# Two 32-byte fillings, a table product moved from GpSimd to VectorE, and three moved steps in a routed attention-and-experts kernel

## Chip, cores and metric

The kernel runs on one core of one Trainium2 chip. The metric is the time of one execution in device microseconds (us), the median of three runs. The profile is of one further execution.

## What is computed

Attention without a softmax (a sigmoid of scaled scores), a layer of eight experts in which every token goes to one expert, and a gated feed-forward layer that all tokens pass. Cut to what matters:

```python
scores = scale * np.matmul(q, k.transpose(0, 1, 3, 2)) - np.log(S)    # 4 x 12 heads, 448 x 448, head 64
attn = 1.0 / (1.0 + np.exp(-scores))
x = np.matmul(attn, v)                       # as x: 1792 tokens x 768
logits = normalized(x) @ normalized(expert_emb).T / tau
expert_idx = np.argmax(logits, axis=1)       # one of 8; gate_w is its softmax weight
for e in range(E):
    out[mask] = gate_w[mask, None] * (np.maximum(x[mask] @ w1[e], 0.0) @ w2[e])   # 768 -> 1024 -> 768
gate = 1.0 / (1.0 + np.exp(-(out @ w_gate)))                                     # 768 -> 1536
y = gate * (out @ w_val) @ w_out                                                 # 1536 -> 768
```

## The kernel before

**Stages.** Attention runs first (to about 157 us of the span), then the experts (to about 463 us), then the feed-forward layer. Each matrix product of the last two stages is made of three products of a number split in two parts, `hi` (rounded to the fast fp32 form, by ScalarE at L215) and `lo` (the rest, by VectorE at L216): hi·hi, lo·hi, hi·lo. Weights arrive by SyncE's DMA in `rawb`, and `split_next` splits one piece of 128x1536 into a ring of four `hi` and four `lo` buffers, one piece per step of TensorE's work. So each engine works through its instructions in the order in which the program writes them, and that order is laid out by hand.

**Which operands TensorE reads at once.** While one product streams its moving operand, the weights of the next are loaded. In `h` (L1022) the moving operand is the ring and the loaded one the tokens `xh`, `xl`. In `y` (L1006 to L1008) it is the ring and `hh`, `hl`. In `gv` (L1240 to L1242) it is `yT`, and the loaded one is the ring. In `o` (L1006 to L1008 again) it is the ring and `gh`, `gl`.

**Where tiles lie.** Pools stand one behind the other in a partition: `const`, `rawb`, the ring, `yT`, the small `ytp` (two buffers tagged "y") and the feed-forward's own from the left, and from the right end inward `xp` (`xg`, `xh`, `xl`), `rt` (the routing tables), `moe` (`hr`, `hh`, `hl`, `yo`) and `small` (`xTq`, `hTq`). A tile's row takes its bytes rounded up to 32. By their sizes, `rawb` begins at byte 21440, the ring at 70592, `yT` at 119744 and `gh` at 150464, all multiples of 64. `xh` begins at 220128, `hh` at 181344 and `xTq` at 170592, all 32 past a multiple of 64.

**Around the first tokens (175 to 260 us).** `place_c` makes the table `am` on VectorE and from it, by `spread` (L604) on GpSimd, the table `spi` of token numbers. `ids_all` sums it on TensorE (`psid`, L611) in the midst of the product `y` of tile 0, and VectorE copies the sums to `idx`, with which GpSimd fetches the tokens of tiles 2 and 3 (`gather`, L859, an indirect DMA into one of two `xg` buffers). In the loop over `y` of tile 1, at its second step, `front(2)` turns tile 2's tokens, `gate_d` sums the gates, and `own_rows` makes a small product `repid` (L742, two instructions), a VectorE copy (L750) and two GpSimd steps, `own_row` (L751) and `moves` (L752). After that loop comes `gather(4)`. At the end of the tile loop's first pass (p = 2) `table_rows` on VectorE makes the tables of the rows to be written, `y_out(0)` and `y_out(1)` scatter the first outputs, and all engines pass a branch round the code of seldom-used tiles (L1165). In the next pass (p = 3) `small_ids` and `gather_small` fetch the tokens of five small tiles, `xq` and `xz`, into the two `xg` buffers, `front_small` (L1099) turns them, and `gather(5)` stands between.

Of the kernel before, what the change touches and what calls it, by code (L numbers as in the profile page):

```python
# [10 lines left out]
F32 = mybir.dt.float32  # L11
# [6 lines left out]
ALU = mybir.AluOpType  # L18
# [4 lines left out]
D = H * HD  # L23
# [3 lines left out]
P = 128  # L27
# [12 lines left out]
NSTAT = 14  # L40
# [67 lines left out]
def routed_kernel(ctx: ExitStack, tc: tile.TileContext, kqP, vP, emb, tau, w1P, w2P, wffP, cst, out):  # L108
    nc = tc.nc
    V, A, G, T, SP = nc.vector, nc.scalar, nc.gpsimd, nc.tensor, nc.sync  # L110

    cpool = ctx.enter_context(tc.tile_pool(name="const", bufs=1))
# [106 lines left out]
    def split_next(ahead=None, hi_eng=None):  # L219
        i = done_split[0]  # L220
        if i >= len(order):
            return
        done_split[0] += 1
        parts[i] = split(raws[raw_of[i]], ring, i, hi_eng=hi_eng)
        j = next((j for j in range(i + 1, len(order)) if order[j][:2] == ("gv", 0) and order[j][2] in direct), None)
        if j == i + 1:
            f = order[j][2]
            for step in range(3):
                decode(f, step)
            if f + 2 in direct:  # L230
                decode_load(f + 2, stage64[f % 2], raws[raw_of[j + 2]])
        it = order[i]
        if i not in nxt:
            return
        free = [i]
        if it[0] in ("w1", "w2") and PA <= it[1] < PA + NA:

            free = [i - 1, i] if it[2] % 2 else []
            for z in free:
                (h_small if it[0] == "w1" else y_small)(it[1] - PA, order[z][2], raws[raw_of[z]])  # L240
        for z in free:
            if ahead is None:
                load(nxt[z])
            else:
                ahead.append(nxt[z])
# [8 lines left out]

    cs = cpool.tile([P, NCONST], F32, name="cs")

    def C(name, rows=P):
        a, b = _COLS[name]
        return cs[:rows, a:b]

    me = ExitStack()
    xp = me.enter_context(tc.tile_pool(name="xp", bufs=2, side="right"))
# [5 lines left out]
    def R(name, shape, dt=F32):  # L268
        return rp.tile(shape, dt, name=name)
# [25 lines left out]
    ids_h = cpool.tile([CP, NT], F16, name="ids_h")  # L295
# [179 lines left out]
    bc3 = lambda a, n: a.unsqueeze(2).to_broadcast([a.shape[0], a.shape[1], n])  # L475
    bct = lambda a, n: a.unsqueeze(1).to_broadcast([a.shape[0], n, a.shape[1]])
    TT, TS, RED = V.tensor_tensor, V.tensor_scalar, V.tensor_reduce

    mx = R("mx", [CP, NT])
    m2 = R("m2", [CP, NT])  # L480
    eq = R("eq", [CP, NT, E])
    oh = R("oh", [CP, NT, E], F16)
# [114 lines left out]
            T.matmul(ps[:, 0, 0:1], bm[:, t, :], am1[:, k, t : t + 1], start=(t == 0), stop=(t == nt - 1))  # L597
        V.tensor_copy(idx01[:, k : k + 1], ps[:, 0, 0:1])

    def spread(am, vals, name):  # L600
        ncol, n = am.shape[2], len(vals)
        r = R(f"sp{name}", [CP, NT, n, ncol], F16)
        for q, v in enumerate(vals):
            G.tensor_tensor(out=r[:, :, q, :], in0=am, in1=bc3(v, ncol), op=ALU.mult)  # L604
        return r.rearrange("p t a b -> p t (a b)")

    def gathered(b, r, name):
# [14 lines left out]
    am = R("am", [CP, NT, NCOL], F16)  # L622
# [44 lines left out]
    gp = {"f": R("gf", [P, NCOL])}  # L667
# [55 lines left out]
    def place_c():  # L723
        ky = R("ky", [P, NCOL], F16)
        V.tensor_copy(ky, tn)
        TT(out=s3, in0=oh, in1=bct(C("e16", CP), NT), op=ALU.mult)
        po = R("po", [CP, NT])
        RED(out=po, in_=s3, axis=AX.X, op=ALU.add)
        ab = R("ab", [CP, NT], F16)
        TT(out=ab, in0=ai, in1=po, op=ALU.add)  # L730
        TT(out=am, in0=bct(ky[:CP], NT), in1=bc3(ab, NCOL), op=ALU.is_equal)
        gp["i"] = spread(am, [ids_h], "i")

    def ids_all():
        ps = gathered(bm, gp["i"], "id")
# [12 lines left out]
    def own_rows():  # L748

        V.tensor_copy(own_row[:, NPAIR:], repeated(idf, "id"))  # L750
        G.tensor_copy(own_row[:, :NPAIR], idx[:, :NPAIR])  # L751
        G.tensor_scalar(out=moves, in0=own_row, scalar1=float(NK), scalar2=None, op0=ALU.is_lt)  # L752
# [103 lines left out]
    def gather(p):  # L856
        xg = xp.tile([P, D], F32, tag="xg", name=f"xg{p}")
        ids = idx01[:, p : p + 1] if p < 2 else idx[:, p : p + 1]
        G.indirect_dma_start(out=xg, out_offset=None, in_=xd if p else xd[: TE * CP],  # L859
                             in_offset=bass.IndirectOffsetOnAxis(ap=ids, axis=0))  # L860
        xg_t[p] = xg

    def front(p, later=None):
        xg = xg_t.pop(p)
        ps = slot(f"xTp{p}")
        psf = ps.rearrange("p a b -> p (a b)")
        for k in range(KD):
            T.transpose(psf[:, k * P : (k + 1) * P], xg[:, k * P : (k + 1) * P], ident)
        if 0 <= p - 1 - PA < NA or p == PZ + 3:
            turn_small(min(p - 1 - PA, NA), psf[:, D : D + 256])  # L870
        hi = xp.tile([P, D], F32R, tag="xh", name=f"xh{p}")
        lo = xp.tile([P, D], F32R, tag="xl", name=f"xl{p}", bufs=1)
        A.copy(hi, psf[:, :D])
        xg_t["T", p] = (hi, lo)
        rest = lambda: V.tensor_sub(lo, psf[:, :D], hi)
        if later is None:
            rest()
        else:
            later.append(rest)
# [186 lines left out]
    def y_scale(p):  # L1066
        yo_t[p] = mp.tile([P, 2, 384], F32, tag="yo", name=f"yo{p}")
        A.activation(yo_t[p], yp_t.pop(p)[:, :, :384], AF.Copy, scale=gate_s[:, p : p + 1])
# [16 lines left out]

    def gather_small():
        for name, n, ids in (("xq", P, idq), ("xz", RQ, idx[:RQ, NCOL - 1 : NCOL])):
            x = xp.tile([P, D], F32, tag="xg", name=name)[:n]
            G.indirect_dma_start(out=x, out_offset=None, in_=xd,
                                 in_offset=bass.IndirectOffsetOnAxis(ap=ids, axis=0))  # L1090
            xg_t[name] = x
# [177 lines left out]
    ytp = ctx.enter_context(tc.tile_pool(name="yt", bufs=2, reuse_waits="tile"))  # L1269
# [36 lines left out]
    for c in range(NW2):  # L1306
        y_chunk(1, c, part[c])
        if c == 1:
            front(2)
            gate_d()  # L1310
            own_rows()
            y_scale(0)
        split_next()
    y_scale(1)

    gather(4)
    YT0, DEC_GAP = 9, 2
    for p in range(2, NSTAT):
        k, r = divmod(p - 4, DEC_GAP)
        dec = r == 1 and 0 <= k < DEC_MOE  # L1320
        if r == 0 and k < DEC_MOE:
            decode_load(DEC_ORDER[DEC_ATT + k], dp.tile([P, 2 * CH], F32, tag="w64", name=f"w64_{k}"),
                        dp.tile([P, CH], F32, tag="w32", name=f"w32_{k}"))
        for c in range(NW1):
            h_chunk(p, c)
            if p == 2 and c == NW1 - 2:
                front(3)
            elif p == 3 and c == 0:
                turn(2)
                small_ids()  # L1330
                gather_small()
            split_next()
            if c == 1 and p - PZ in (0, 1, 3):
                small_step((0, 2, 0, 6)[p - PZ])
            if dec and c % 2 == 0:
                decode(DEC_ORDER[DEC_ATT + k], c // 2)
        if 2 < p < NSTAT - 2:
            gather(p + 2)
        if 3 < p + 1 < NSTAT:
            front(p + 1)  # L1340
        if p > 2:
            for c in range(NW2):
                y_chunk(p - 1, c)
                if c == 2 and YT0 < p <= YT0 + 4:
                    yT_unit(0, p - YT0 - 1)
                split_next()
                if c == 1 and PZ <= p < PZ + 4:
                    small_step((1, 3, 4, 7)[p - PZ])
                if c == 3 and p == PZ + 2:
                    small_step(5)  # L1350
                if dec and c == 1:
                    decode(DEC_ORDER[DEC_ATT + k], 2)
            y_out(p - 1)
        else:
            table_rows()
            y_out(0)
            y_out(1)
            tail = [yTp.tile([P, KD, 512], F32R, tag=f"yT{k}", name=f"tail{k}") for k in range(2)]
            tail += [dp.tile([P, 6, 512], F32, tag="w64", name="tail_w"),
                     dp.tile([P, CH], F32, tag="w32", name="tail_x"), slot("tail")]  # L1360
            tc.mark_branch_hint_location("beyond", hint='LikelyTaken', engines=[mybir.EngineType.PE])
            n_tiles = nc.values_load(tabs["n"], min_val=0, max_val=NPAIR)
            tail_tiles(NSTAT)
        if p > 2:
            turn(p)
        if p == 3:
            front_small()
            gate_e()
        if p in (4, 5, 6):
            (packed_a, packed_b, packed_c)[p - 4]()  # L1370
        if YT0 <= p < YT0 + 4:
            y_load(G, 0, p - YT0)
        if p == PZ - 2:
            decp.close()
            dp = decp.enter_context(tc.tile_pool(name="zw", bufs=1, side="right", reuse_waits="tile"))
            for k in range(3):
                load_small(k)
# [118 lines left out]
```

## Time and profile before

| | us |
|---|---|
| median of three runs (1007.59 to 1008.35) | 1008.24 |
| the profiled execution | 1004.97 |
| its span, first to last instruction | 1003.2 |
| TensorE busy with products | 986.2 (98%) |
| VectorE busy | 584.2 (58%) |
| ScalarE busy | 484.5 (48%) |
| GpSimd busy | 108.8 (11%) |

The profiled execution lies 3.3 us below the median. A busy TensorE is one with a product under way: how close together products start is seen only in the order of time. PE is TensorE, PEld its weight loads, DVE VectorE, ACT ScalarE, POOL GpSimd, SP SyncE; a q behind a name is the engine's sequencer.

### The profile page before, as it was taken

How to read it: one execution, taken by the hardware profiler on the slowest of the kernel's cores; microseconds unless marked ns; L12 is line 12 of the kernel's file. 1: busy time of each engine (PE TensorE's matmuls, PEld its weight loads, DVE VectorE, ACT ScalarE, POOL GpSimd, SP SyncE). 2: the span in 40 equal slices, each digit the busy share in tenths (PEclk: the TensorE clock that was granted, in tenths of full speed). 3: DMA queues.
4: the chain of work that ended last, by engine and by line, in shares of the span. 5: the costliest groups of instructions: out<-in, count | busy, mean ns of one | idle time of the engine just before them, and what ended most of it. 6: DMA issues, size and time to landing. Idle time of an engine off the chain costs nothing.

```text
span 1003.2 us, 15168 instructions
## 1 busy us (share of the span) xinstructions
PE 986.2 (98%) x6099; PEld 815.4 (81%) x6099; DVE 584.2 (58%) x660; ACT 484.5 (48%) x527; POOL 108.8 (11%) x102
## 2 busy tenths in 40 slices
PE   9999999898999999999999999999999999999998
PEld 4455556777877788889888899888899888899998
DVE  6877768778887777876588633333333333322652
ACT  6676776485666677775322422333322333322441
POOL 0011013403331121201000000000000000001000
PEclk9999999998999999999999999999999999999999
DMA  8999875556699974692668633333333323323640
GB/s 304 319 360 333 294 247 173 186 195 240 231 382 319 317 287 156 214 326 78 231 211 295 215 109 114 130 100 105 135 106 117 130 100 106 134 86 114 217 154 32
DMA packets 40061, 198.21 MB, mean 198 GB/s; under 512 B 5048, under 2 KB 7624, under 8 KB 37552
## 3 DMA queue, kind: packets, MB, share of 16 engines
q1 hardware_dynamic: 32160, 159.46, 46.2%
q0 software_dynamic: 7824, 37.72, 9.9%
q8 instruction: 48, 0.79, 0.3%
q14 instruction: 29, 0.24, 0.1%
HBM read 197.46 MB, written 31.16 MB: 228 GB/s over the span
## 4 chain that ended last, share of the span: by engine, by line
PE 75%; DMA 2%; issue 1%; DVE 0%; ACT 0%; POOLq 0%
PE gv L1241 12%; PE gv L1240 11%; PE gv L1242 11%; PE h L1022 8%; PE o L1008 6%; PE o L1006 6%; PE o L1007 6%; PE y L1006 3%; PE y L1008 3%; PE y L1007 3%; PE qh L1111 2%; PE qy L1134 1%; DMA xg<-xd,idx 1%; PE hTp L1041 1%; PE yTp L1226 1%
## 5 line engine op out<-in xcount | busy, mean ns | idle before, releaser
L216 DVE TENSOR_TENSOR lo<-rawb,hi 128x1536 fp32r<-128x1536 f32 x176 | 307.7, 1758 | 295.4 <-ACT hi L215 292.8
L215 ACT CAST hi<-rawb 128x1536 fp32r<-128x1536 f32 x174 | 256.5, 1479 | 250.9 <-PE gv L1241 97.3
L1242 PE MATMUL gv<-yT,lo 128*128 128x512 f32 (+1 forms) x576 | 209.0, 363 | 0.0
L1240 PE MATMUL gv<-yT,hi 128*128 128x512 f32 (+1 forms) x576 | 209.0, 363 | 0.0
L1241 PE MATMUL gv<-yT,hi 128*128 128x512 f32 (+1 forms) x576 | 208.9, 363 | 0.0
L1240 PEld LDWEIGHTS gv<-yT,hi 128*128 128x128 f32 x576 | 108.8, 189 | 16.8
L1242 PEld LDWEIGHTS gv<-yT,lo 128*128 128x128 f32 x576 | 108.8, 189 | 16.8
L1241 PEld LDWEIGHTS gv<-yT,hi 128*128 128x128 f32 x576 | 108.7, 189 | 16.7
L1006 PE MATMUL o<-hi,gh 128*128 128x384 f32 x336 | 112.8, 336 | 0.0
L1008 PE MATMUL o<-lo,gh 128*128 128x384 f32 x336 | 112.4, 334 | 0.0
L1007 PE MATMUL o<-hi,gl 128*128 128x384 f32 x336 | 112.3, 334 | 0.0
L381 ACT ACTIVATE attn<-sc,bias_s 128x896 f32<-128x896 f32 x84 | 79.0, 1003 | 28.5 <-PE sc L379 28.2
L1405 ACT CAST gh<-sg 128x512 fp32r<-128x512 f32 (+1 forms) x48 | 27.2, 567 | 129.8 <-DVE sg L1404 129.8
L1006 PE MATMUL y<-hi,hh 128*128 128x384 f32 x208 | 73.3, 353 | 1.5 <-DVEq L1165 1.5
L1008 PE MATMUL y<-lo,hh 128*128 128x384 f32 x208 | 71.6, 344 | 1.4 <-DVE lo L216 1.4
L1007 PE MATMUL y<-hi,hl 128*128 128x384 f32 x208 | 71.6, 344 | 0.9 <-DVE hl L1047 0.8
L393 PE MATMUL av<-attn,v 128*64 128x448 f32 (+1 forms) x384 | 70.7, 545 | 0.3 <-DVE xT L398 0.2
L1022 PE MATMUL h<-hi,xh 128*128 128x512 f32 x168 | 68.6, 408 | 0.2
L1022 PE MATMUL h<-lo,xh 128*128 128x512 f32 x168 | 66.4, 395 | 0.0
L1007 PEld LDWEIGHTS o<-hi,gl 128*128 128x128 f32 x336 | 63.1, 188 | 0.1
L1006 PEld LDWEIGHTS o<-hi,gh 128*128 128x128 f32 x336 | 63.1, 188 | 0.1
L1008 PEld LDWEIGHTS o<-lo,gh 128*128 128x128 f32 x336 | 63.1, 188 | 0.0
(316 smaller groups left out, 1185.3 us busy)
## 6 DMA issues: line engine op xcount, KB each, us to landing
rawb<-wd SPq DMA_DIRECT2D x65, 768.0 KB
rawb<-in_w1P SPq DMA_DIRECT2D x52, 768.0 KB
rawb<-in_w2P SPq DMA_DIRECT2D x52, 768.0 KB
rawb<-in_wffP SPq DMA_DIRECT2D x16, 1536.0 KB
wd<-rawb POOLq DMA_DIRECT2D x16, 768.0 KB, 7.4
kq<-in_kqP SPq DMA_DIRECT2D x24, 448.0 KB
xd<-xr_sb POOLq DMA_DIRECT2D x12, 336.0 KB, 7.0
y<-yd SPq DMA_DIRECT2D x10, 384.0 KB
```

Source lines behind the costliest of these rows:

```text
L215: (hi_eng.tensor_copy if hi_eng else A.copy)(hi, raw)
L216: V.tensor_sub(lo, raw, hi)
L381: A.activation(at_, ps[:, :, :S], AF.Sigmoid, bias=bias_s, scale=1.0 / math.sqrt(HD))
L393: T.matmul(av_t[j * HD : (j + 1) * HD, i % 2, :S], v[rows, j * HD : (j + 1) * HD], at_[rows, j, :], start=(u == first_unit(i)), stop=(u == ...
L1006: T.matmul(o, ah[:, ks], bh[:, w], start=(k == 0), stop=False)
L1007: T.matmul(o, al[:, ks], bh[:, w], start=False, stop=False)
L1008: T.matmul(o, ah[:, ks], bl[:, w], start=False, stop=(k == nk - 1))
L1022: T.matmul(ps[:, half, :], x[:, k * P : (k + 1) * P], w[:, s * 512 : (s + 1) * 512], start=(k == 0 and x is xh and w is hi), stop=(k == KD ...
L1240: T.matmul(o, hi[:, a, k, :], yh[:, k, :n], start=(k == 0), stop=False)
L1241: T.matmul(o, hi[:, a, k, :], yl[:, k, :n], start=False, stop=False)
L1242: T.matmul(o, lo[:, a, k, :], yh[:, k, :n], start=False, stop=(k == KD - 1))
L1405: A.copy(gh[:, f, :n], sg[:, :n])
```

## The change

Two tiles of 32 bytes that nothing uses are allocated, one in `const` behind the constants, one in `rt` behind its first tile. The product `spi` is issued on VectorE. `own_rows` is issued after the loop over `y` of tile 1 and ahead of `y_scale(1)`. `xq` and `xz` get the two "y" buffers of `ytp`. `gather(5)` is issued in pass 2 behind `front(3)`, no longer in pass 3.

```diff
@@ -254,6 +254,8 @@
     cs = cpool.tile([P, NCONST], F32, name="cs")
 
+    cpool.tile([P, 8], F32, name="fill_c")
+
@@ -477,6 +479,7 @@
     mx = R("mx", [CP, NT])
+    R("fill_r", [P, 8])
     m2 = R("m2", [CP, NT])
@@ -597,11 +600,11 @@
-    def spread(am, vals, name):
+    def spread(am, vals, name, eng=G):
         ncol, n = am.shape[2], len(vals)
         r = R(f"sp{name}", [CP, NT, n, ncol], F16)
         for q, v in enumerate(vals):
-            G.tensor_tensor(out=r[:, :, q, :], in0=am, in1=bc3(v, ncol), op=ALU.mult)
+            eng.tensor_tensor(out=r[:, :, q, :], in0=am, in1=bc3(v, ncol), op=ALU.mult)
         return r.rearrange("p t a b -> p t (a b)")
@@ -729,7 +732,7 @@
-        gp["i"] = spread(am, [ids_h], "i")
+        gp["i"] = spread(am, [ids_h], "i", V)
@@ -1085,7 +1088,7 @@
         for name, n, ids in (("xq", P, idq), ("xz", RQ, idx[:RQ, NCOL - 1 : NCOL])):
-            x = xp.tile([P, D], F32, tag="xg", name=name)[:n]
+            x = ytp.tile([P, D], F32, tag="y", name=name)[:n]
@@ -1308,9 +1311,9 @@
         if c == 1:
             front(2)
             gate_d()
-            own_rows()
             y_scale(0)
         split_next()
+    own_rows()
     y_scale(1)
 
     gather(4)
@@ -1325,6 +1328,7 @@
             if p == 2 and c == NW1 - 2:
                 front(3)
+                gather(5)
             elif p == 3 and c == 0:
@@ -1334,7 +1338,7 @@
-        if 2 < p < NSTAT - 2:
+        if 3 < p < NSTAT - 2:
             gather(p + 2)
```

## Rows read from the trace of the kernel before

**Rows 1.** Stretches (us: busy us and count per engine, clock, DMA share, GB/s).

```profile
200.00:250.00 50.00, 44.87 (x217) 38.06 (x216) 39.00 (x45) 34.83 (x30) 9.96 (x8) 0.93 0.60 217
```

**Rows 2.** Waits of TensorE: who waited for whom, us in total, times, longest.

```profile
PE psid L611 <- POOL spi L604: 2.2, 1, 2.2
PE xTp L868 <- DMA xg<-xd,idx: 2.0, 2, 1.3
...
PE repid L742 <- DVE xl L875: 1.3, 1, 1.3
```

**Rows 3.** GpSimd's groups, 174 to 260 us: busy us, mean ns | idle before.

```profile
L604 POOL TENSOR_TENSOR spi<-am,ids_h 112x416 f16<-112x416 f16 x1 | 4.0, 3992 | 9.8 <-DVE am L731 9.8
...
L604 POOL TENSOR_TENSOR spg<-am,g 112x416 f16<-112x416 f16 x3 | 2.7, 884 | 4.0 <-DVE g L810 3.7
```

**Rows 4.** VectorE in order of time, 180 to 226 us (start, us, instruction).

```profile
180.94 0.59 DVE L731 TENSOR_TENSOR am<-ky,ab 112x416 f16<-112x416 f16 x1
181.45 3.42 DVE L216 TENSOR_TENSOR lo<-rawb,hi 128x1536 fp32r<-128x1536 f32 x2
186.25 0.18 DVE L736 CAST idx<-psid 128x26 int32<-128x26 f32 x1 [1.38 <-PE psid L611]
...
190.39 1.23 DVE L1047 TENSOR_TENSOR hl<-hTp,hh 128x1024 fp32r<-128x1024 f32 x1 [2.28 <-ACT hh L1046]
...
201.54 5.09 DVE L216 TENSOR_TENSOR lo<-rawb,hi 128x1536 fp32r<-128x1536 f32 x3 [2.26 <-ACT hi L215]
```

**Rows 5.** ScalarE in order of time, 186 to 224 us.

```profile
188.14 0.31 ACT L801 ACTIVATE sh<-sh 112x128 f32<-112x128 f32 x1 [5.09 <-DVE sh L798]
189.34 1.01 ACT L1046 CAST hh<-hTp 128x1024 fp32r<-128x1024 f32 x1 [0.89 <-PE hTp L1041]
```

**Rows 6.** TensorE in order of time, 180 to 230 us.

```profile
191.67 0.44 PE L1007 MATMUL y<-hi,hl 128*128 128x384 f32 x1
...
221.89 0.82 PE L868 MATMUL xTp<-cs,xg 128*128 128x128 f32 x6
224.22 0.42 PE L1006 MATMUL y<-hi,hh 128*128 128x384 f32 x1 [1.52 <-DVEq L1165]
```

**Rows 7.** GpSimd in order of time, 194 to 260 us.

```profile
200.16 1.04 POOL L859 DMA_INDIRECT xg<-xd,idx  x1 [0.38 <-issue]
...
239.75 2.16 POOL L859 DMA_INDIRECT xg<-xd,idx  x1 [6.45 <-PE xTq L1099]
```

**Rows 8.** The fourteen fetches into `xg`: issue to landing.

```profile
DMA to landing us min/median/max: 3.9/6.4/10.2
```

**Rows 9.** TensorE's groups by form: count | busy us, mean ns.

```profile
L1240 PE MATMUL gv<-yT,hi 128*128 128x512 f32 x432 | 168.2, 389 | 0.0
...
L1008 PE MATMUL o<-lo,gh 128*128 128x384 f32 x336 | 112.4, 334 | 0.0
...
L1007 PE MATMUL y<-hi,hl 128*128 128x384 f32 x208 | 71.6, 344 | 0.9 <-DVE hl L1047 0.8
...
L1022 PE MATMUL h<-lo,xh 128*128 128x512 f32 x168 | 66.4, 395 | 0.0
```

**Rows 10.** Chain that ended last: one unbroken run of `h` (start, us, count).

```profile
263.49 8.40 PE h L1022 x36
```

**Rows 11.** TensorE in time: first and last of runs (`y` 18, `o` 27, `gv` 42 apart).

```profile
257.16 0.34 PE L1006 MATMUL y<-hi,hh 128*128 128x384 f32 x1
...
260.34 0.34 PE L1006 MATMUL y<-hi,hh 128*128 128x384 f32 x1
...
577.96 0.33 PE L1006 MATMUL o<-hi,gh 128*128 128x384 f32 x1
...
582.64 0.34 PE L1006 MATMUL o<-hi,gh 128*128 128x384 f32 x1
...
640.43 0.39 PE L1240 MATMUL gv<-yT,hi 128*128 128x512 f32 x1
...
649.95 0.39 PE L1240 MATMUL gv<-yT,hi 128*128 128x512 f32 x1
```

## The prediction

> **What bounds the kernel now.** I read the stretches first, then TensorE's waits, then the engines in order of time around each wait, and last TensorE's products by form. TensorE is the bound nearly everywhere: of the span of 1003.2 us it is busy for 986.2. The stretch of 200 to 250 us is the exception, with 44.87 us busy and a mean granted clock of 0.93 [rows 1]. There are thus two ways to gain: take out waits of TensorE, some 17 us in all, or make its products follow each other more closely. The change tries both, and the two have little to do with each other. The waits that it touches are three: 2.2 us for `spi`, 1.3 us for a VectorE step ahead of the small product `repid`, and the longer, 1.3 us, of two waits for tokens fetched into `xg` [rows 2]. A fourth, at the first product of `y` of tile 2, isn't touched by any edit: TensorE had turned tile 4's tokens at 221.89 and went on at 224.22, when VectorE had passed the branch L1165 [rows 6].
>
> **The table on VectorE.** On GpSimd `spi` took 3.99 us, though three products of the same shape took 0.88 each later [rows 3]; the first ran beside VectorE's `lo`. On VectorE the nearest row is `am` just ahead of it: the same shape and type, 0.59 us [rows 4]. So `spi` would be there at about 182.1, before TensorE asks for it (2.2 us ahead of where it went on), and the wait goes. But VectorE's own queue now counts. Behind `spi` stand two `lo`, 3.42 us without a pause, and then `idx`: 182.1 + 3.4 is 185.5, against 186.25 before, 0.75 earlier and not 2.2 [rows 4]. What follows `idx` there ends in the table that ScalarE raises to the exponential at 188.14, so at 187.4 now, for 0.31; behind it stands `hh`, which waited for TensorE until 189.34 [rows 5]. TensorE's transposes come 2.2 earlier (187.1), so `hh` begins behind the exponential, at 187.7: 1.64 earlier. `hl` follows as before (1.05 us after `hh` begins), and the second product of `y` of tile 1, which stood at 191.67 directly behind `hl` [rows 4, 6], comes 1.6 earlier. **1.6 us**, then; 2.2 if `hl` weren't late, and about 1 if the product takes VectorE 1.2 us. VectorE's extra 0.6 is otherwise covered: the two `lo` behind it are for products after the `psid` sums, and those products had them already.
>
> **The small product moved.** `repid` waited 1.3 us because VectorE had not yet emptied the PSUM buffer that it takes over [rows 2]. Behind the loop, half of `y` of tile 1 later (24 products at 0.177, 4.2 us), that buffer is long empty and its own operand `idf` too; its two instructions cost the same there. **1.3 us**; below that by as much as a different buffer would be late. Each step of `own_rows` is moved past others: the VectorE copy falls in behind three `lo` that ended at 206.63 [rows 4], and GpSimd, in order, holds `moves` and then `gather(4)` until that copy. `gather(4)`, sent at 200.16 [rows 7], would be sent at 207.5 at the latest. The longest of fourteen such fetches took 10.2 us [rows 8]: landed by 217.7. Its reader stood at 221.89 [rows 6] and comes some 2.9 us earlier, at 219.0. So 1.3 us is spare in the worst case and 5 at the median landing of 6.4; without that cover, each us late would be a us of the end. `moves` is read by `table_rows`, later than that copy by 10 us.
>
> **The small tokens' buffers and the sixth fetch.** These are one step in two lines. `xq` and `xz` held both `xg` buffers, so `gather(5)` stood for 6.45 us until TensorE had turned `xq`, went out at 239.75 [rows 7] and took 10.2 us to land, the maximum [rows 8]. TensorE waited 1.3 us for it [rows 2]. With `xq` and `xz` in the `ytp` buffers, last used by attention and next for the first `y` loads six passes on, and `gather(5)` sent behind `front(3)`, it lands some 30 us before it is read. On GpSimd it stands ahead of `y_out(0)`, which waits 13 us longer for its table, and costs it 1 us of issuing there. **1.3 us**. Next late in that place would be `lo` of the coming `y`, done 2 us or more ahead.
>
> These three sum to 4.2 us. What would eat it is the fourth wait: if VectorE reached the branch no earlier than before, the 2.9 us of the first two would be waited there. VectorE's last `lo` ahead of `table_rows` follow `xl` of tile 3, which has one buffer and so waits for TensorE's end with tile 2's `h`. It follows TensorE, and I take the fourth wait as unchanged. [...]
>
> **The fillings.** They add no instruction; they move tiles by 32 bytes. `fill_c` moves all from the left: the ring, `rawb`, `yT`, `gh`, `gl` from a multiple of 64 bytes to 32 past one. `fill_r` moves the pools inward of `rt`: `hh`, `hl`, `xTq` from 32 past to a multiple of 64. `xp` lies outside and stays 32 past. Does a start matter? VectorE and DMAs I price at nothing. For TensorE there is a difference in the rows. Means of one product are 395 ns in `h` against 389 in `gv`, both of 512 columns, and 344 in `y` against 334 in `o`, both of 384 [rows 9]. The spacing says it more cleanly: `h` 8.40 us / 36 = 233.3 ns [rows 10], `gv` 9.52 / 42 = 226.7, `y` 3.18 / 18 = 176.7, `o` 4.68 / 27 = 173.3 [rows 11]. In `gv` and `o` moving operand and loaded weights both start on a multiple of 64; in `h` and `y` the ring does, and the loaded one starts 32 past. So 6.6 ns per product of 512 and 3.4 per one of 384 go with starts that differ. After the change they are alike in `h` (both 32 past), differ the other way round in `y`, and are alike in `gv` and `o` (both 32 past). No row shows both 32 past, or `y`'s new pairing. The ends for `h` are nothing and 504 x 6.6 ns = 3.3 us gained, and I take 3.3: in a pair read at the same time, what differs is likelier to be how the two streams meet than where one starts. For `y` the ends are 0 and 624 x 3.4 = 2.1 us gained; I take 0, by today's `y`. For `gv` and `o` they are 0 and, should the start alone decide, 1296 x 6.6 + 1008 x 3.4 = 12.0 us lost; I take 0.
>
> [...]
>
> **Sum.** 4.2 + 3.3 = 7.5 us: the profiled execution's 1004.97 would become 997.5. It lies 3.3 us below the median, so against the median of 1008.24 I say **1000.7 us**.
>
> **Rivals.**
> (a) The fillings do nothing: `h` and `gv` differ by something else, say that `h` changes PSUM halves every three products. Against it, `y` and `o` read the same ring slices in the same order. 1008.2 - 4.2 = 1004.0.
> (b) Slower: the weights' own start decides, 32 past being the dear one. Then `y` gains 2.1, `h` stays, `gv` and `o` lose 12.0: 1008.2 - 4.2 + 9.9 = 1013.9. It is slower than before as soon as a third of the products in `gv` and `o` are dearer. For it: the rows fit it as well as mine. Against it: the extra is larger for the longer stream, 6.6 to 3.4, while the loaded weights are the same size.
> (c) The first two waits come back at the branch: 1008.2 - 1.3 - 3.3 = 1003.6. For it: VectorE, ScalarE and GpSimd's queues are all moved past there.
> (d) All waits come back and the fillings do nothing, or the edits just don't do what they say: 1008.2.
> (e) The moving operand's start is dear too: all of `h`, `y`, `gv` and `o` lose, 17.4 us in sum, 1021.4. Or the new starts are better everywhere, by as much: 986.6.
>
> **How the numbers follow.** Forecast 0.42, (a) 0.20, (b) 0.13, (c) 0.10, (d) 0.08, (e) 0.07 (0.04 slower, 0.03 faster). About 0.2% (2 us) is what a measurement of this kernel can tell from no change. Faster by more: forecast, (a), most of (c), the better half of (e): 0.72; I give (c) 0.07 of its 0.10. Same: (d) and the rest of (c), 0.11. Slower: (b) and the worse half of (e), 0.17. The forecast's own range is 996.5 (should `y` gain 2.1 and the clock 2) to 1003. The range takes in (a), (c) and (d): 996.5 to 1010, leaving out (b) and (e), 0.20.
>
> **What would show it.** Right: no wait on `spi`, `repid` or `xg` beyond some 0.3 us; `hl` late by half a us in `y` of tile 1; `gather(5)` issued near 208; the fourth wait as long as before; runs of 36 `h` in 8.16 us, `gv` still 42 in 9.52 and `o` 27 in 4.68. Wrong: `gv` at 233 ns (then (b)), `h` at 233 (then (a)), or a longer stall at 220 (then (c)).

## The result: 9.3 us faster, and what the profile after shows

The median fell from 1008.3 (1008.24 with one run fewer, as above) to 998.82 us. The ratio, taken over all runs, is 0.9908 (0.9890 to 0.9927), which is 9.3 us. Measured once more beside the experiments it was 0.9900 (0.9885 to 0.9915), with a median of 998.07. The profiled execution after has a span of 999.1 us and took 1000.87, 2.0 us above its median, while that of before lay 3.3 below its own. The two traces are therefore only 4.1 us apart. 2.8 us of what is missing is attention, in which no step of the change lies: TensorE's first transposes of tokens stand at 158.93 us after and at 156.12 before, and in the 14 traces of this case anywhere from 155.75 to 158.93, at 157.2 on average. From them to the end, before took 847.1 us and the change 840.2: 6.9 less.

First TensorE's waits after the change (who waited for whom, us in total, times, longest). None on `spi`, `repid` or a late `xg` is left [rows 2]; the 0.8 us on `xg` is tile 1's fetch near 170 us, the shorter of the two of before. The three waits at `y` of tile 2 are all there, and one of 0.8 for `hl` has come in `y` of tile 1.

```profile
PE y L1011 <- DVE lo L216: 1.7, 1, 1.7
PE y L1010 <- DVE hl L1050: 1.6, 2, 0.8
PE y L1009 <- ACT hr L1037: 1.5, 1, 1.5
...
PE xTp L871 <- DMA xg<-xd,idx: 0.8, 1, 0.8
```

VectorE in order of time after the change (start, us, instruction). `spi` takes 0.59 us directly behind `am`, where GpSimd took 3.99 [rows 3, 4]. The two `lo` stand behind it, and `hl` has become late by its wait for `hh`.

```profile
183.75 0.59 DVE L734 TENSOR_TENSOR am<-ky,ab 112x416 f16<-112x416 f16 x1
184.38 0.59 DVE L607 TENSOR_TENSOR spi<-am,ids_h 112x416 f16<-112x416 f16 x1
184.89 3.42 DVE L216 TENSOR_TENSOR lo<-rawb,hi 128x1536 fp32r<-128x1536 f32 x2
188.23 0.18 DVE L739 CAST idx<-psid 128x26 int32<-128x26 f32 x1
...
191.35 1.23 DVE L1050 TENSOR_TENSOR hl<-hTp,hh 128x1024 fp32r<-128x1024 f32 x1 [1.28 <-ACT hh L1049]
```

TensorE in order of time: `psid` now begins 0.18 us behind the product before it. Tile 4's tokens are turned at 221.28 and `y` of tile 2 begins at 223.64: 2.36 us, against 2.33 before [rows 6].

```profile
185.62 0.34 PE L1011 MATMUL y<-lo,w 128*128 128x384 f32 x1
185.80 0.57 PE L614 MATMUL psid<-spi,bm 112*128 112x26 f16 x16
...
221.28 0.82 PE L871 MATMUL xTp<-cs,xg 128*128 128x128 f32 x6
223.64 0.41 PE L1009 MATMUL y<-hi,hh 128*128 128x384 f32 x1 [1.54 <-ACT hr L1037]
```

GpSimd in order of time: `moves` waits for VectorE's copy, `gather(4)` goes out at 209.71 and `gather(5)`, the second line with `xg`, at 212.20, where it went at 239.75 before [rows 7].

```profile
207.82 1.62 POOL L755 TENSOR_SCALAR moves<-own_row 128x26 f32<-128x26 f32 x1 [9.51 <-DVE own_row L753]
209.71 2.19 POOL L862 DMA_INDIRECT xg<-xd,idx  x1 [0.27 <-PE xTp L871]
212.20 0.96 POOL L862 DMA_INDIRECT xg<-xd,idx  x1 [0.30 <-PEq L1168]
```

One unbroken run of 36 products of `h`, from the chain that ended last, is 8.21 us long (228.1 ns each) and was 8.40 [rows 10]. `gv` has the same mean as before [rows 9].

```profile
261.75 8.21 PE h L1025 x36
```

```profile
L1243 PE MATMUL gv<-yT,hi 128*128 128x512 f32 x432 | 168.2, 389 | 0.0
```

The stretch around `y` of tile 2, by windows (us: busy us and count per engine, clock, DMA share, GB/s): between 225 and 233 us TensorE's mean granted clock was 0.57. For 6.8 us of it the clock stood at the lower of its two levels (0.50 of full speed; the other is 1.00), as it did for 6.8 us around there before.

```profile
200.00:250.00 50.00, 45.65 (x226) 39.49 (x225) 39.04 (x47) 35.48 (x30) 11.87 (x9) 0.93 0.65 234
225.00:233.00 8.00, 6.30 (x20) 6.05 (x21) 7.96 (x8) 2.07 (x2) 3.28 (x3) 0.57 0.25 85
```

### The profile page after: what moved, and what is told of

It reads as the page before. It is cut to its first block, busy times and chain, and to the rows that moved or that the text cites. A ratio compares the mean times of both kernels' runs of the same rounds, so it can differ in the third digit from the quotient of the medians.

```text
span 999.1 us, 15166 instructions
## 1 busy us (share of the span) xinstructions
PE 982.5 (98%) x6099; PEld 813.9 (81%) x6099; DVE 584.4 (58%) x661; ACT 484.4 (48%) x527; POOL 106.9 (11%) x101
## 4 chain that ended last, share of the span: by engine, by line
PE 77%; DVE 0%; ACT 0%; issue 0%
PE gv L1245 12%; PE gv L1244 12%; PE gv L1243 12%; PE h L1025 8%; PE o L1011 6%; PE o L1010 6%; PE o L1009 6%; PE y L1009 4%; PE y L1011 3%; PE y L1010 3%; PE qh L1114 2%; PE qy L1137 1%; PE hTp L1044 1%; PE yTp L1229 1%; PE xTp L871 1%; DVE lo L216 0%
```

## Experiments

The theory: the moved steps take away three waits (4.2 us by the forecast), the fillings bring TensorE's products closer together (3.3 us), and the two add up. Times are medians, gains in us go by the ratio. Spacings are means of the distance from start to start between neighbouring products of one form, taken where neither waited (200 to 245 ns for 512 columns, 160 to 190 for 384): some 450 pairs for `h`, some 600 for `y`.

| kernel | us | ratio to before |
|---|---|---|
| the change | 998.82, 998.07 | 0.9908, 0.9900 |
| fillings alone | 1005.05 | 0.9964 (0.9950 to 0.9978) |
| moved steps alone | 1001.11 | 0.9926 (0.9912 to 0.9940) |
| `spi` alone | 1004.67 | 0.9974 (0.9958 to 0.9990) |
| the change and a hint for VectorE's branch | 1002.81 | 0.9947 (0.9933 to 0.9960) |

The others were run once, for their traces: filling in `const` 1004.59, in `rt` 1006.61, `own_rows` 1005.40, sixth fetch 1008.64, fillings of 64 bytes 1006.02, the two with a filling at the right end 999.36 and 1000.05.

**The fillings alone.**

```diff
+    cpool.tile([P, 8], F32, name="fill_c")
+    R("fill_r", [P, 8])
```

> The two fillings alone, none of the three moved steps. The trace after the change has products of h 227 ns apart (233.3 before), of y 174 (176.7), and gv and o unchanged at 226.7 and 173.3. If these come from the fillings, this kernel shows the same four spacings, keeps the three waits (spi about 2.2 us, repid 1.3, xg 1.3), and is faster by 504 x 6.3 ns = 3.2 us for h and 624 x 2.7 ns = 1.7 us for y, together 4.9 us, a ratio near 0.995. Rival one: the spacings come with the moved steps; then they stay at 233 and 177 here, and the ratio is 1.000. Rival two: the fillings bring more than TensorE's spacing, because attention's tiles move too; then the ratio is 0.993 or lower and the time to the first tile of tokens is shorter than in the kernel before by 2 us or more.

Measured: 3.6 us (2.2 to 5.0) at 0.9964. `h` 228.5 ns (233.0 before), `y` 174.4 (176.6), `gv` 226.8 and `o` 173.5 as before. 504 products by 4.5 ns are 2.3 us, 624 by 2.2 are 1.4: 3.7. So the spacings come from the fillings, and they account for the gain within its interval; both rivals fall (attention took 157.91 us, not 2 less). TensorE's waits and two windows:

```profile
PE psid L614 <- POOL spi L607: 2.8, 1, 2.8
PE xTp L871 <- DMA xg<-xd,idx: 2.7, 2, 2.2
...
PE repid L745 <- DVE xl L878: 1.3, 1, 1.3
```

```profile
184.00:189.00 5.00, 2.21 (x27) 1.98 (x26) 3.52 (x8) 0.28 (x1) 3.89 (x2) 1.00 0.92 313
189.00:192.00 3.00, 3.00 (x13) 2.91 (x12) 0.79 (x4) 0.31 (x1) 1.55 (x2) 0.51 0.86 342
```

The three waits stand, two of them longer than in the profile of before (2.8 for 2.2, 2.2 for 1.3) [rows 2]. And there is something that profile doesn't have: behind the wait for `spi`, in which TensorE was busy for 2.21 of 5 us, it runs for 3.4 us at the lower level of its clock (0.51 over the 3 us of the second window), though it is busy without a pause (3.00 of these 3 us).

**The moved steps alone.** The diff is that of the change without its two fillings.

> The three moved steps alone, without fillings. By the forecast's terms: no wait on spi, repid or xg, 1.6 + 1.3 + 1.3 = 4.2 us gained, a ratio near 0.996, with the products of h still 233 ns apart and of y 177. The two parts would then add up: about 4.9 us of the fillings and 4.2 of this make 9.1. Rival: the first two gains are given back at the wait ahead of y of tile 2, as TensorE stood there as long as before in the trace after; then 1.3 us, a ratio of 0.999, and that wait is 2.9 us longer than before.

Measured: 7.5 us (6.0 to 8.9), not 4.2. The spacings are those of before (`h` 233.0, `y` 176.7), so nothing of it is TensorE's pace. The rival falls: the waits at `y` of tile 2 are 1.5, 0.8 and 1.7 us, against 1.5, 0.8 and 1.4 before. One wait is new, for the small tokens:

```profile
PE xTq L1099 <- DMA xz<-xd,idx: 2.1, 1, 2.1
PE y L1008 <- DVE lo L216: 1.7, 1, 1.7
PE y L1006 <- DVEq L1165: 1.5, 1, 1.5
```

```profile
184.00:192.00 8.00, 7.42 (x59) 6.91 (x58) 6.34 (x18) 1.23 (x3) 2.03 (x3) 1.00 0.87 297
224.00:232.00 8.00, 6.46 (x29) 6.46 (x30) 8.00 (x6) 3.38 (x4) 3.57 (x3) 0.79 0.12 49
```

The first window has the full clock, where the fillings alone had 0.51 for 3 us. In the second the low stretch is half as long as after the change (3.4 us; 0.79 over 8 us against 0.57).

**`spi` alone.** It asks whether the low clock belongs to the wait.

```diff
-        gp["i"] = spread(am, [ids_h], "i")
+        gp["i"] = spread(am, [ids_h], "i", V)
```

> Only the product spi moved to VectorE. The three kernels above that keep spi on GpSimd show, behind its wait of 2.2 to 2.8 us, a stretch of 3.4 us at a granted clock of 0.5 that begins at 185 to 189 us; the kernel with the moved steps and the profiled execution before don't. Theory: the wait costs itself and the low clock behind it. Then this kernel has no wait on spi and no low stretch near 186, waits about 0.65 us longer for hl in y of tile 1, and gains 1.6 + 1.7 = 3.3 us, a ratio near 0.997. Rival: the low stretch has nothing to do with the wait; it is there in this profile too, and the gain is 1.6 us, a ratio of 0.9984.

Measured: 2.6 us (1.0 to 4.2). The value lies between the two theories and the interval reaches to both, so the time doesn't decide. The trace does better: no wait on `spi`, and the full clock behind it.

```profile
PE y L1007 <- DVE hl L1047: 1.6, 2, 0.8
...
PE repid L742 <- DVE xl L875: 1.3, 1, 1.3
```

```profile
184.00:192.00 8.00, 7.77 (x59) 6.85 (x57) 6.48 (x14) 2.38 (x3) 2.00 (x2) 1.00 0.88 312
```

Over all traces: of seven with `spi` on GpSimd, five have the low stretch of 3.4 us within 6 us of the wait (both fillings of either size, each filling alone, the sixth fetch alone), two don't (before, `own_rows` alone). Of the seven with `spi` on VectorE none has it. It costs 1.2 to 1.6 us; in the fillings alone, for one, `psid` and the first `y` behind the transposes are 4.95 us apart, and 3.40 in the trace of before. The wait's length doesn't decide it: it was 2.2 us both in before and with the filling in `rt`, and 2.5 with `own_rows` alone. The mean granted clock of the untraced executions points the same way. Of 37 executions of before beside the experiments 25 had 0.995 or less, and they were 0.7 to 1.2 us longer on average than the others of their series; of the 26 of `spi` alone, the moved steps alone and the change none had less than 0.996.

**`own_rows` alone.**

```diff
             gate_d()
-            own_rows()
             y_scale(0)
         split_next()
+    own_rows()
```

> Only own_rows moved behind the loop. Forecast: no wait of 1.3 us at repid, which stands behind the last y of tile 1; the fetch of tile 4 goes out at about 207 to 209 us and lands before TensorE asks for it at about 219; the wait ahead of y of tile 2 stays 1.5 us and the two behind it 0.8 and 1.4. Rival: VectorE comes to the branch no earlier, and that first wait becomes 2.8 us. The wait on spi (2.2 us or more) and that on the tokens fetched last into xg (1.3 us or more) stay.

Measured: no wait at `repid`. Between `psg` and the first `y` of tile 2 this trace gains 1.26 us on that of before, and the wait ahead of that `y` is 1.4 us: kept, not given back. `gather(4)` goes out at 209.07 and lands at 218.90; its reader comes at 220.99, so 2.1 us are spare. The two other waits are again longer than in the profile of before:

```profile
PE xTp L868 <- DMA xg<-xd,idx: 2.5, 2, 2.1
PE psid L611 <- POOL spi L604: 2.5, 1, 2.5
```

**The sixth fetch alone.**

```diff
-            x = xp.tile([P, D], F32, tag="xg", name=name)[:n]
+            x = ytp.tile([P, D], F32, tag="y", name=name)[:n]
...
                 front(3)
+                gather(5)
...
-        if 2 < p < NSTAT - 2:
+        if 3 < p < NSTAT - 2:
```

> Only the small tokens' buffers and the sixth fetch. Forecast: no wait for xg near 250 us (1.3 us in the profile before, 1.9 to 2.4 us in the three kernels above that keep the old order), all else as before. Rival: the small tokens now come too late, as in the run of all three steps, where TensorE waited 2.2 us for xz near 236 us; then that much is lost again here. What speaks against it: in this kernel TensorE reaches that place 2 to 3 us later than there, while xz goes out at about the same time.

Measured: the wait near 250 us is gone (1.46 us gained there on the trace of before), and nothing waits for `xz`: it landed at 239.93, its reader came at 244.52. The single time of 1008.64 says nothing against it: this execution lost 2.1 us on that of before in attention between 70 and 90 us, and had the low clock behind `spi`.

```profile
PE psid L611 <- POOL spi L604: 2.6, 1, 2.6
PE y L1006 <- ACT hr L1034: 1.8, 1, 1.8
PE y L1008 <- DVE lo L216: 1.7, 1, 1.7
PE repid L742 <- DVE xl L875: 1.3, 1, 1.3
```

**Where the tiles begin.** Five kernels test the rule of the forecast (starts that differ are dear) against its rivals. First each filling by itself:

> Only the filling in const: the ring, yT, gh and gl begin 32 bytes past a multiple of 64, and xh, xl, hh, hl stay 32 past one too; all pairs alike. Theory one (the forecast's: starts that differ are dear): h 226.7 ns, y 173.3, gv and o unchanged. But the trace after has y at 174 with starts that differ the other way round. Theory two (only one pairing is dear: the streamed operand at a multiple of 64 and the loaded one 32 past): the same here. Theory three (each tile's own start decides, hh and hl being cheaper at a multiple of 64): y stays at 176.7 here, and h stays at 233.3, since xh and hh haven't moved.

> Only the filling in rt: hh and hl begin at a multiple of 64, as the ring does; xh and xl stay 32 past one with the ring at a multiple. Theories one and two: h stays at 233.3 ns, y falls to 173.3. If h falls to 227 here too, the pairing of starts isn't the cause; if y stays at 176.7, what made y faster is the ring's move and not its own.

then both with `[P, 16]` in place of `[P, 8]`:

> Both fillings with 64 bytes in place of 32: the ring, yT, gh, gl, hh and hl all move by 64 bytes and keep their place against a multiple of 64. If the start against a multiple of 64 is what counts, nothing changes: h 233.0 ns on average, y 176.6. If it is the mere move, or the start against a multiple of 128, then h and y change: the ring now begins on a multiple of 128, hh and hl 32 past one, xh 96 past one.

and, with the moved steps, a filling at the right end of the partition, outside `xp`, in place of both, and in place of that in `rt`:

```diff
+    ep = me.enter_context(tc.tile_pool(name="edge", bufs=1, side="right"))
+    ep.tile([P, 8], F32, name="fill_e")
     xp = me.enter_context(tc.tile_pool(name="xp", bufs=2, side="right"))
```

> The moved steps, and in place of the two fillings one of 32 bytes at the right end of the partition: xh, xl, hh and hl all begin on a multiple of 64, as the ring does; yT, gh and gl stay on one. This is the forecast's own rule put to the test with the other pair of equal starts. If equal starts are what counts, h falls to 227 to 228.5 ns (233.0 before) as it did with both 32 past; if it is the ring's start alone, h stays at 233. y (hh moved, ring not) should repeat the 175.9 of the kernel with the filling in rt alone.

> The moved steps, the filling in const and the one at the right end, without that in rt: the ring, yT, gh and gl begin 32 past a multiple of 64, and xh, xl, hh and hl on one. By the forecast's rule (starts that differ are dear) h is 233 ns here. If the ring's start alone counts for h, 228.4, as in the changed kernel; if the loaded tile's start counts as well, as it does for y, which is at its lower value with this pairing (174.4), h falls below 228.4, to 226.8 at the least, the spacing of gv. y should stay at 174.4.

Measured (bytes past a multiple of 64 of ring, `xh`, `hh`; then how far `hh` lies above the ring's first buffer):

| kernel | ring, `xh`, `hh` | `h` ns | `y` ns | `hh` - ring |
|---|---|---|---|---|
| before | 0, 32, 32 | 233.0 | 176.6 | 110752 |
| moved steps alone | 0, 32, 32 | 233.0 | 176.7 | 110752 |
| filling in `const` | 32, 32, 32 | 228.3 | 176.0 | 110720 |
| filling in `rt` | 0, 32, 0 | 233.0 | 175.9 | 110720 |
| right end | 0, 0, 0 | 228.2 | 175.8 | 110720 |
| the change | 32, 32, 0 | 228.4 | 174.4 | 110688 |
| `const` and right end | 32, 0, 0 | 233.1 | 173.9 | 110688 |
| both by 64 bytes | 0, 32, 32 | 233.2 | 173.8 | 110624 |

The runs of 36 `h` in the chain that ended last, in the order of the filling in `const`, in `rt`, both by 64 bytes, right end, and `const` with right end:

```profile
422.24 8.18 PE h L1024 x36
```

```profile
423.92 8.40 PE h L1023 x36
```

```profile
423.66 8.40 PE h L1025 x36
```

```profile
259.74 8.19 PE h L1024 x36
```

```profile
259.78 8.39 PE h L1026 x36
```

For `h` the forecast's rule holds in all four pairings: both at a multiple of 64 or both 32 past, 228.2 to 228.5; one of each, either way round, 233.0 to 233.2. Neither tile's own start matters. For `y` the rule is wrong: equal starts give 175.8 to 176.0, differing ones 173.8 to 174.4, or 176.6 and 176.7, and a move by 64 bytes, which leaves every start against a multiple of 64 as it was, is worth 2.8 ns. What orders the eight rows is the distance between the two tiles: where it is the same the spacing is within 0.5 ns, wherever the tiles begin, and over these four distances it falls as the distance falls. For `h` too it can be read as the distance (`xh` 149504 bytes above the ring is the fast one, 149472 and 149536 the slow): in these kernels to begin alike and to lie 149504 bytes apart are the same thing, so the runs don't part the two. A kernel has many pairs, since ring, `xh` and `xl`, `hh` and `hl` follow each other in steps of 3072, 4096 or 6144 bytes; all of these are multiples of 1024, so the pairs of one kernel share the distance's rest by 1024. That rest is 0 for the fast `h` and, in every kernel here, for `gv` and `o`, whose spacing never changed; for `y` it is 160, 128, 96 and 32, and no run put it at 0. Why it matters, and whether it goes on like this, the runs don't show. A fifth to a quarter of the `h` products in the fast kernels still stand 231 to 236 ns apart, which is why the gain is 4.6 ns and not 6.6.

**The wait that the change left.** The changed kernel with the branch hint, which TensorE alone had, given to VectorE too, ahead of `table_rows`:

```diff
+            tc.mark_branch_hint_location("beyond", hint='LikelyTaken',
+                                         engines=[mybir.EngineType.PE, mybir.EngineType.DVE])
             table_rows()
             y_out(0)
...
-            tc.mark_branch_hint_location("beyond", hint='LikelyTaken', engines=[mybir.EngineType.PE])
```

> The changed kernel with one thing more: the hint for the branch round the seldom-used tiles, which so far only TensorE gets, is given to VectorE too, and ahead of table_rows. In the trace after the change VectorE ends its last step of table_rows at 220.20 us and begins hl at 223.58, with nothing but the branch between; TensorE, which has the hint, loses 0.46 us at its own. Theory: the three waits of TensorE ahead of and in y of tile 2 (1.5, 0.8 and 1.7 us) hang on VectorE's branch. Then hl begins near 220.7, the first lo behind it ends near 223.7, TensorE's third product comes at about 223.8 in place of 226.99, and some 3 us are gained; up to 3.4 more if the low clock of 6.8 us behind these waits goes with them. Against the kernel before a ratio of 0.985 to 0.988. Rival: the wait is ScalarE's, which ends hr at 223.53; then the first product stays at 223.6, and with hl and lo long done the gain is the same 3 us, so that the row of hl tells which. Rival two: the hint doesn't shorten VectorE's branch; hl still begins 3.4 us behind table_rows and the ratio is that of the changed kernel, 0.991.

Measured: 1002.81 us, 4.7 slower than the changed kernel beside it. The hint does its work: `hl` begins 1.1 us behind `table_rows` and not 3.4, and TensorE has no wait ahead of `y` of tile 2; that of 1.7 us for `lo` stays. Between tile 4's transposes and the third product of `y` 3.4 us pass, 5.7 in the change: 2.3 us gained there, not 3. So the first theory is right as to who was late. Its time is wrong: the next late thing, the fetch of the small tokens, stood 12 us on. VectorE around the branch, GpSimd's fetch of the small tokens, SyncE's next weight loads with the hint and then in the change, TensorE's waits, and two windows:

```profile
218.20 0.16 DVE L786 SCALAR_TENSOR_TENSOR rowq<-rb,cs 128x5 int32<-128x5 f32 x1
219.47 1.23 DVE L1050 TENSOR_TENSOR hl<-hTp,hh 128x1024 fp32r<-128x1024 f32 x1 [1.11 <-DVEq L1168]
```

```profile
229.47 1.75 POOL L1092 DMA_INDIRECT xq<-xd,idq  x1 [4.12 <-DVE xl L878]
```

```profile
230.40 5.34 SPq L172 DMA_DIRECT2D rawb<-in_w1P  x4
```

```profile
234.51 4.85 SPq L172 DMA_DIRECT2D rawb<-in_w1P  x3
```

```profile
PE xTq L1102 <- DMA xq<-xd,idq: 4.8, 1, 4.8
PE y L1011 <- DVE lo L216: 1.7, 1, 1.7
...
PE xTq L1102 <- DMA xz<-xd,idx: 0.8, 1, 0.8
```

```profile
225.00:235.00 10.00, 7.00 (x44) 6.73 (x42) 10.00 (x7) 7.38 (x6) 4.53 (x5) 1.00 0.45 152
235.00:246.00 11.00, 8.40 (x28) 6.82 (x29) 1.68 (x3) 2.43 (x2) 1.22 (x1) 0.53 1.00 375
```

TensorE is ready for the small tokens at 232.00, but `xq`, sent at 229.47, lands at 236.67, and `xz` at 239.06. GpSimd stands for 4.1 us between the second scatter of `y_out` and that fetch, with the branch between them, in this trace as in that of the change (4.13). TensorE's wait of 4.8 us is followed by 10.2 us at the lower clock (0.53 over the 11 us of the last window). In the change this doesn't show: there `xz` landed at 234.86 and was read at 239.39. Counted from tile 4's transposes, TensorE is ready 4.8 us sooner with the hint (12.6 against 17.4; there is no low clock on the way), and `xq` lands 4.4 later (17.2 against 12.9). Had it landed as in the change, TensorE would have waited some 0.3 us for it. The fetch was longer under way: 7.2 us for `xq` and 7.5 for `xz`, against 4.3 and 3.4. What had changed around it is the weight loads of the next expert step (`in_w1P`), which were issued while `xq` was under way, and 0.4 us behind its landing in the change. With the moved steps alone TensorE came 2.7 us sooner than in the first trace of the change, these loads were issued at 233.05 with `xz` under way since 231.75, `xz` took 7.0 us, and TensorE waited 2.1. In the twelve other traces they come 0.3 to 0.5 us behind `xq`'s landing, `xq` took 3.9 to 4.7 us and `xz` 3.3 to 3.5. That the loads lengthen the fetch is read from this order in 14 traces; no run moved them alone.

**The change again.**

> The changed kernel as it is, beside the others on the same chip. From its first measurement 0.991; from the parts timed above, 0.9964 for the fillings and 0.9926 for the moved steps, the product is 0.989. If it comes out above 0.991, the parts take something from each other. In the profile: no wait on spi, repid or xg; whether the low clock behind y of tile 2 lasts 3.4 us (as with the moved steps alone) or 6.8 (as in the first profile).

Measured: 0.9900, beside 0.989 from the product of the parts; they add up. No wait on `spi`, `repid` or a late `xg`; the low stretch behind `y` of tile 2 is the long one again:

```profile
222.00:230.00 8.00, 6.30 (x20) 6.05 (x21) 7.96 (x8) 2.27 (x3) 3.31 (x3) 0.57 0.24 84
```

## Why the prediction was right, and where its terms were not

The forecast was 1000.7 us, 7.5 faster; it became 998.8 and 998.1, faster by 9.3 and 10.1 by the ratios. The mechanisms were the ones named; three sizes were off, and so was the step from one execution to the median. Against the trace that the sum was worked out from, it was close: behind the first transposes of tokens the two traces of the change are 6.9 and 7.0 us shorter, against 7.5.

**The table on VectorE: right in every row, too small in the sum.** The product takes 0.59 us, the wait is gone, and `hl` gives part of it back, as said. In the two traces TensorE gains 2.6 us from tile 1's transposes up to `psid` and loses 0.8 by the product behind `hl`: 1.8 with a little of the closer products in it, against 1.6. The step that failed is the last one of the sum, which carried the waits of one execution over to the median. That execution lay 3.3 us below the median. Some 1.1 of this is attention (156.12 us against 157.2 on average), which the change leaves alone. But of seven with `spi` on GpSimd it is also one of two without the low clock behind this wait (1.2 to 1.6 us), and the other six show waits for `spi` of 2.2 to 2.8 where it showed 2.2. The fillings alone show what that comes to: behind the first transposes their trace is no shorter than that of before (847.4 us against 847.1), though its products are 3.7 us closer. The forecast subtracted all 3.3 us as if they had nothing to do with the waits in question. How they divide in the untraced executions isn't shown.

In all seven traces with `spi` on GpSimd it takes 3.99 or 4.00 us there, ends some 0.7 us behind VectorE's two `lo` of 3.42 beside it, and the same shape took 0.88 elsewhere [rows 3, 4]. Why it takes longer beside them no run shows.

**The small product moved: right.** 1.5 us in the two traces and 1.26 alone, against 1.3. `gather(4)` was sent at 209.71 rather than 207.5 and landed 1.7 us ahead of its reader; the worst case of the forecast left 1.3.

**The sixth fetch: right, too small.** 1.65 us in the two traces and 1.46 alone, against 1.3. It lands at 220.46, 28 us ahead of its reader. But in five other traces with the old order this wait had 1.7 to 2.2 us, in one 0.1; 1.3 was again what one execution happened to show.

**The fourth wait: right.** 2.36 us between the transposes and `y` of tile 2, against 2.33. That it is set by VectorE's branch was said; that it also kept TensorE and the weight loads behind the small tokens' fetch was not.

**The fillings: right by two errors.** `h` was to gain 3.3 us and gained 2.3, its rule holding in all four pairings, but not for all products: the size was worked out as if each would then stand 226.7 ns from the next. `y` was to gain nothing and gained 1.4. That the sum of 3.7 comes near the forecast's 3.3 is luck. Rule (b), that the loaded tile's own start decides, fell as well. `gv` and `o` stayed as said, so that rival (b) of 1013.9 and both halves of (e) didn't occur.

Rival (a), fillings that do nothing, doesn't go with the spacings of `h` and `y`, which moved with the tiles (233.0 to 228.5 ns, 176.6 to 174.4).

Rival (c), waits that come back at the branch, didn't occur in any trace. A wait of that kind came later, at the small tokens, and shows in the moved steps alone (2.1 us) and with the hint (4.8).

Still open: why the low clock behind `y` of tile 2 lasted 3.4 us in the trace of the moved steps alone and 6.8 in the twelve other traces with that wait, that of before among them. The 2 us that the forecast's range counts for the clock are shown by no run; the two traces of the change have the same 6.8 us there as that of before. The fillings don't decide how long it lasts: of the four executions of the change measured again, the traced one had a mean granted clock of 0.996 and the other three 0.998, as had all six of the moved steps alone. No kernel run here is shown to beat the change: the filling at the right end in place of both (999.36 in its one run) has `h` as close and `y` 1.4 ns further apart.

## What to carry to other kernels

Look at where the profiled execution stands to the median before taking the size of a wait from it: one that is 3 us below it can have the short version of just those waits that vary, and a wait can bring a stretch at the lower clock that isn't in its own row (here 3.4 us behind the wait for `spi`, in five of seven traces). When a wait is taken out, search for the next transfer that the time gained runs into, and for what else then starts sooner; here 2.3 us gained ahead of one product brought TensorE and the next weight loads into a fetch 12 us on, and the kernel became 4.7 us slower. Where TensorE streams one tile and loads another, compare start-to-start distances of products of one shape across stages: differences of about 2% hung here on where the two tiles lie.

## What the hardware showed that was not expected

- The spacing of `h` was 228.2 to 228.5 ns where both tiles begin alike against a multiple of 64 bytes (or, the same thing here, lie 149504 bytes apart) and 233.0 to 233.2 where not; that of `y` went with the tiles' distance (173.8 to 176.7 ns) and not with that.
- VectorE stood 3.38 us at a branch round code that isn't run without a hint and 1.11 with one.
- A fetch of the small tokens took 3.3 to 4.7 us from issue to landing, and 7.0 to 7.5 where the next weight loads were issued while it was under way (two traces).
- TensorE's wait of 2.2 to 2.8 us for `spi` was followed in five of seven traces by 3.4 us at the lower of its two clock levels (0.51 over 3 us with the fillings alone, where full speed is 1.00), though TensorE was busy by then; that of 4.8 us for `xq` by 10.2 us (0.53 over 11 us).
- `spi`, 0.59 us on VectorE, took 3.99 or 4.00 on GpSimd in each of seven traces beside VectorE's `lo`.
